# A fused attention and two-MoE kernel: attention's 1206 steps in another written-out order, with some steps on another engine

## The chip, the cores and the metric

The kernel runs on one NeuronCore of a Trainium2 chip, as one program in one launch. The core has five engines that run side by side, each working through its own queue of instructions in order: TensorE (PE in the profile; PEld is its weight load), VectorE (DVE), ScalarE (ACT), GpSimd (POOL) and SyncE (SP, which here only starts transfers). An engine goes on when the semaphores that its next instruction waits for have been raised by the others. The metric is the device time of one execution in microseconds (us); lower is better.

## What is computed

```
scores = q @ k.T / sqrt(D), causal mask       # B=4, H=8, S=576, D=64, all fp32
local  = softmax(scores) @ v
q_p    = phi(q)                               # elu(q) + 1
mem    = (q_p @ M_prev) / (q_p . z_prev + 1e-6)
a      = g * mem + (1 - g) * local            # g = sigmoid(beta) of each head
x = a as [2304 tokens, 512]
x = leaky_relu(x @ w_in) @ w_out              # 512 -> 2048 -> 512, slope 0.01
x = (x @ w_a * (x @ w_b)) @ w_out2            # 512 -> 1536 -> 512
```

## The kernel before

The two MoE layers do every fp32 product as three products of split operands: a high part and a low part of each side, and high x high + high x low + low x high are summed (`three`, lines 286 to 288). They run over groups of 256 hidden columns and over the tokens in two parts (1024 and 1280), and what stands in them is not touched by the change. The change lies in `attention`, which runs first.

**Attention.** It works on 16 pairs of heads, called w = 0 to 15; two pairs in a row (w even and odd) share the work called phi. For each pair:

- `scores` (L578) multiplies q and k of two heads at once. D is 64, so each head takes half of TensorE's rows: the array stands in a mode of 64 rows. Blocks of 128 queries have 128, 256, 384 or 512 keys. `scores_tail` (L606) does the last 64 queries of two pairs in a mode of 64 x 64.
- `least` (L586, L616) on VectorE adds the mask and takes the row minimum of the negated scores out of PSUM; `exp_of` (L532) on ScalarE makes the exponentials and their sum; `recip` (L543, L547) on VectorE inverts the sums; `norm` (L559), on VectorE or GpSimd, multiplies the probabilities by them and by 1 - g.
- `probs_T` (L637) transposes the probabilities on TensorE with the full array, 128 x 128 at a time, and ScalarE or VectorE copies the result out of PSUM (L336, L338) into the tiles `early`, `late` and `tail`.
- `phi` (L452 to L492) makes q_p and its normalisation for two pairs: a minimum (L452), an exponential (L455), `high` (L458), a product with z (`times`, L463 and L468), its sum (`total`, L473), a reciprocal (L487) and a scaling (L343). `phi_T` (L509) transposes it.
- `pv_memory` (L688) and `pv_local` (L716) sum the memory and the local part in the same PSUM banks; the 28 matmuls of `pv_local` stand in a mode of 64 columns, for two heads side by side. `store` copies the result into `xf`; `halves_of` splits it into the high and low parts `xh` for the first token part.
- Beside these stand the first two weight tiles (`Weights.micro`, four half tiles of nine steps each) and the first four accumulations of the MoE layer (`first`, four steps of three matmuls for each).

**What sets the order.** Each piece of work is a step given to a `Plan` by `add` or `dma`, with the engines that could do it and a cost for each. The order is not computed: the table `ORDER` names all 1206 steps, each with a letter for its engine (A ScalarE, D VectorE, E TensorE, G GpSimd, S SyncE), and `run` issues them in that order; each engine's queue is the sub-sequence with its letter. What the engines then wait for follows from the tiles that a step reads and writes. The costs (`TURN`, `COLD`, `took`, `timed`) only give each step a planned start, and from the planned starts of TensorE's steps `run` works out one thing: how many matmuls on the mask (`spin`, L310, results never read) it puts into TensorE's gaps ahead of the first `pv_local`. Costs flagged `port` belong to VectorE steps that the planner treats as sharing a memory port with GpSimd.

Of the kernel before, what the change touches and what calls it, by code (L numbers as in the profile page):

```python
# [19 lines left out]
B, H, S, D = 4, 8, 576, 64  # L20
# [10 lines left out]
def chunks(pr):  # L31
# [13 lines left out]
COLD = 1400.0, 7000.0  # L45
# [1158 lines left out]
```

## Time and profile before

| | |
|---|---|
| time of three runs | 1036.42, 1037.19, 1037.19 us, median 1037.19 |
| span of the profiled execution (first to last instruction) | 1034.8 us |
| what the median holds beyond the span | 2.4 us |
| attention, up to the first matmul of the layers' own loop | 0 to 204.4 us |
| the two MoE layers | 204.4 us to the end |
| steps on TensorE, VectorE, ScalarE, GpSimd, SyncE in attention | 264, 396, 355, 142, 49 |

The profiled execution's own time is not listed apart from the three runs; its span is. Sums are made on the span, and the 2.4 us between it and the median are added at the end. Busy time is the time in which an engine has an instruction in hand; ends of matmuls are modelled, so TensorE's busy share also holds short waits between matmuls.

### The profile page before, as it was taken

The numbers are of one execution on the slowest core, as the hardware profiler recorded it, in microseconds if no ns is written. First come the engines' busy times: TensorE is split into PE (matmuls) and PEld (weight loads), VectorE is DVE, ScalarE is ACT, GpSimd is POOL, SyncE is SP. The second block draws the span as 40 slices with busy tenths as digits, with TensorE's granted clock in tenths as the row PEclk, the third lists the DMA queues.
The fourth block names the chain that finished last, engine by engine and source line by source line (L and its number), as shares of the span: only waits on it lengthen the run. The fifth ranks groups of instructions, "written<-read, shape, count | busy, mean of one in ns | idle before, by whom it ended". The sixth has DMA issues, their size and how long they took to land.

```text
span 1034.8 us, 14335 instructions
## 1 busy us (share of the span) xinstructions
PE 1025.3 (99%) x5420; PEld 826.8 (80%) x5420; DVE 700.4 (68%) x1377; ACT 394.3 (38%) x910; POOL 360.3 (35%) x325
## 2 busy tenths in 40 slices
PE   9999999999999999999999999999999999999998
PEld 4566666788888888888888888888888888888887
DVE  7999998497675758475666683862963955945334
ACT  6899998564323222222323342412122112211111
POOL 4666675135344444342524031420420421411000
PEclk9999999999999999999999999999999999999999
DMA  7334431112111111111101010210210210200022
GB/s 237 117 103 135 145 125 60 57 47 82 41 62 42 61 41 62 41 47 35 62 23 59 1 61 21 82 41 1 82 42 1 82 42 21 82 21 1 1 82 101
DMA packets 19605, 63.31 MB, mean 61 GB/s; under 512 B 2384, under 2 KB 3152, under 8 KB 19536
## 3 DMA queue, kind: packets, MB, share of 16 engines
q1 hardware_dynamic: 19392, 62.40, 17.6%
q8 instruction: 42, 0.69, 0.3%
q14 instruction: 27, 0.22, 0.1%
q10 hardware_dynamic: 144, 0.00, 0.0%
HBM read 57.68 MB, written 4.72 MB: 60 GB/s over the span
## 4 chain that ended last, share of the span: by engine, by line
PE 92%; DVE 6%; ACT 1%; DMA 0%; POOL 0%; issue 0%; ACTq 0%; DVEq 0%; POOLq 0%
PE b L286 27%; PE b L288 27%; PE b L287 27%; PE b L716 3%; PE b L637 3%; PE b L578 2%; DVE p L586 2%; ACT p L532 1%; PE b L688 1%; PE b L509 1%; DVE phi L458 1%; DVE qraw L463 0%; DVE nr L473 0%; PE b L606 0%; DVE pt L616 0%; DMA raw<-in_kqT 0%
## 5 line engine op out<-in xcount | busy, mean ns | idle before, releaser
L286 PE MATMUL b<-xh,w 128*128 128x512 f32 (+1 forms) x800 | 295.4, 369 | 0.0
L287 PE MATMUL b<-xh,w 128*128 128x512 f32 (+1 forms) x800 | 294.6, 368 | 0.0
L288 PE MATMUL b<-xh,w 128*128 128x512 f32 (+1 forms) x800 | 294.4, 368 | 0.0
L225 POOL TENSOR_TENSOR wa<-wa,w 128x512 f32<-128x512 f32 x64 | 108.7, 1698 | 497.6 <-DVE wh L219 399.8
L288 PEld LDWEIGHTS b<-xh,w 128*128 128x128 f32 x800 | 150.8, 188 | 25.3
L286 PEld LDWEIGHTS b<-xh,w 128*128 128x128 f32 x800 | 150.9, 189 | 24.9
L287 PEld LDWEIGHTS b<-xh,w 128*128 128x128 f32 x800 | 150.9, 189 | 24.9
L214 ACT CAST w<-wa 128x512 fp32r<-128x512 f32 x68 | 42.2, 620 | 224.2 <-DVE wa L206 220.0
L1061 DVE TENSOR_TENSOR gf<-b,gf 128x512 f32<-128x512 f32 (+1 forms) x60 | 38.1, 636 | 125.6 <-PE b L288 125.6
L964 DVE TENSOR_TENSOR hl<-gf,hl 128x512 fp32r<-128x512 f32 (+1 forms) x66 | 51.3, 778 | 76.0 <-ACT hl L963 75.6
L1027 DVE TENSOR_TENSOR xf<-b,xf 128x512 f32<-128x512 f32 (+1 forms) x140 | 87.1, 634 | 19.3 <-PE b L288 17.2
L228 POOL TENSOR_TENSOR w<-wa,wr 128x512 fp32r<-128x512 f32 x66 | 92.1, 1396 | 7.0 <-DVE wa L225 1.4
L963 ACT CAST hl<-gf 128x512 fp32r<-128x512 f32 (+1 forms) x91 | 52.5, 577 | 91.0 <-DVE gf L1061 89.5
L1004 ACT ACTIVATE gf<-b 128x512 f32<-128x512 f32 (+1 forms) x76 | 42.0, 553 | 108.5 <-PE b L288 107.0
L286 PE MATMUL b<-hl,w 128*128 128x512 f32 (+1 forms) x220 | 81.1, 368 | 0.0
L287 PE MATMUL b<-hl,w 128*128 128x512 f32 (+1 forms) x220 | 81.0, 368 | 0.0
L288 PE MATMUL b<-hl,w 128*128 128x512 f32 (+1 forms) x220 | 80.9, 368 | 0.0
L559 POOL TENSOR_SCALAR p<-p,stat,keep 128x384 f32<-128x384 f32 (+3 forms) x92 | 61.2, 678 | 47.6 <-DVE stat L547 22.7
L1059 ACT COPY gf<-b 128x512 f32<-128x512 f32 (+1 forms) x60 | 32.5, 542 | 115.7 <-PE b L288 114.9
L532 ACT ACTIVATE p<-p,stat 128x384 f32<-128x384 f32 (+3 forms) x128 | 71.4, 563 | 7.0 <-DVE stat L586 6.8
L1084 DVE TENSOR_TENSOR xf<-b,xf 128x512 f32<-128x512 f32 (+1 forms) x91 | 60.8, 680 | 18.7 <-PE b L288 18.3
L199 DVE TENSOR_SCALAR wh<-wraw 128x512 uint32<-128x512 uint32 x68 | 63.4, 933 | 0.0
(119 smaller groups left out, 1760.7 us busy)
## 6 DMA issues: line engine op xcount, KB each, us to landing
wraw<-in_w_in SPq DMA_DIRECT2D x16, 512.0 KB, 3.4
wraw<-in_w_out SPq DMA_DIRECT2D x16, 512.0 KB, 3.3
qraw<-in_qn SPq DMA_DIRECT2D x8, 768.0 KB, 6.2
wraw<-in_w_a SPq DMA_DIRECT2D x12, 512.0 KB, 3.4
wraw<-in_w_b SPq DMA_DIRECT2D x12, 512.0 KB, 3.3
wraw<-in_w_o SPq DMA_DIRECT2D x12, 512.0 KB, 3.4
vs<-in_vn SPq DMA_DIRECT2D x16, 320.0 KB, 2.9
raw<-in_kqT SPq DMA_DIRECT2D x16, 288.0 KB, 4.4
```

What stands on the lines that cost most here:

```text
L199: nc.vector.tensor_scalar(u("h"), self.raw[i][:, :, 1], 0x7FFFFFFF, None, ALU.bitwise_and)
L225: (nc.gpsimd if eng == "POOL" else nc.vector).tensor_tensor(t["a"], t["a"], f32(half(0)), ALU.subtract)
L228: (nc.gpsimd if eng == "POOL" else nc.vector).tensor_tensor(half(1), t["a"], t["r"], ALU.add)
L286: nc.tensor.matmul(outp, l_hi, r_hi, start=start, stop=False)
L287: nc.tensor.matmul(outp, l_hi, r_lo, start=False, stop=False)
L288: nc.tensor.matmul(outp, l_lo, r_hi, start=False, stop=stop)
L532: nc.scalar.activation(t, t, AF.Exp, bias=s[:, 0, col : col + 1], scale=-1.0, accum_out=s[:, 1, col : col + 1])
L559: ENG[eng].tensor_scalar(live[p], live[p], stats[w % 3][:, 3, col : col + 1], k, ALU.mult, ALU.mult)
L963: after(1, lambda: nc.scalar.copy(t[:, 0, c], gf))
L964: after(1 if eng is nc.vector else 2, lambda: eng.tensor_tensor(t[:, 1, c], gf, f32(t)[:, 0, c], ALU.subtract))
L1027: nc.vector.tensor_tensor(y[pr][:, dm, c], op[:, 0:n], y[pr][:, dm, c], ALU.add)
L1084: nc.vector.tensor_tensor(y[:, i, c], op, y[:, i, c], ALU.add)
```

## The change

The table `ORDER` is replaced as a whole: the same 1206 steps, in another order, and 158 of them on another engine. The counts go from before to after: VectorE 396 to 411, ScalarE 355 to 315, GpSimd 142 to 167, TensorE 264 and SyncE 49 as before. Of the 144 `norm` steps GpSimd has 111 in place of 101; of `times` 12 of 16 in place of 6, of `low` 6 in place of 2, of `scale` 10 in place of 8. Of the 128 copies of transposed probabilities VectorE has 40 in place of 11, and of the 32 of `phi_T` 10 in place of none. The planner's costs change too; as the order is written out, they act only through the number of mask matmuls, which goes from 30 to 20. The same transfers are issued, in another order on SyncE.

```diff
-COLD = 1400.0, 7000.0
+COLD = 1500.0, 7000.0
+READY = {"ACT": 3700.0, "DVE": 600.0, "PE": 1500.0, "POOL": 3600.0, "SP": 720.0}
 ...
 ORDER = (
-    'S0 A2 D3 S1 D6 S7 G4 D5 S8 S11 S71 E27 S9 S10 D34 S113 D30 A35 E36 D28 A31 D32 A29 E41 D37 D39 A38 D42 A33 '
 ...
+    'S0 S1 S7 S8 S10 A2 S9 S11 S113 S71 D3 G6 G4 E27 D34 A35 D32 E36 D30 A33 D28 A31 D53 D39 A29 D37 D54 A40 E41 '
 ...
         def dma(self, fn, size, r=(), w=(), at=0.0, count=1, behind=()):
-            self.add(fn, {"SP": 630.0 * count if count > 1 else 475.0}, r, w, at, size, behind, count)
+            self.add(fn, {"SP": 550.0 * count if count > 1 else 475.0}, r, w, at, size, behind, count)
 ...
             if self.locks(i, e):
-                self.shared = end
+                self.shared = end - (200.0 if e == "POOL" else 150.0)
 ...
-            free = dict.fromkeys(("ACT", "DVE", "PE", "POOL", "SP"), 600.0)
+            free = dict(READY)
 ...
-                free[e] = done[i] = start[i] + cost[e]
+                free[e] = done[i] = start[i] + cost[e] * (2 if e == "PE" and start[i] < COLD[1] else 1)
 ...
-                    wire = max(wire, start[i] + cost[e] / count + 650.0) + size / (220.0 if count == 1 else 150.0)
-                    done[i] = wire + 900.0
+                    wire = max(wire, start[i] + cost[e] / count + 650.0) + size / 330.0
+                    done[i] = wire + 1000.0
 ...
-                    busy = t + self.steps[i][1]["PE"]
+                    busy = t + self.steps[i][1]["PE"] * (2 if t < COLD[1] else 1)
```

Left out of this cut: in `load_first` the factor 4 in the planned sizes of the first two transfers becomes 9.

**TensorE, behind the second `pv_local`.** These are the rows from the last transposes of the pair w = 1 (`pt`, `phi`) over the scores of w = 3 (L578, two heads in two banks) to the first transposes of w = 2. Before:

```order
L637 MATMUL b_646<-ident,pt_491 128x128 x4
L509 MATMUL b_655<-ident,phi_329 128x128 x4
L578 MATMUL b_663<-raw_93 128x256
L578 MATMUL b_664<-raw_93 128x256
L509 MATMUL b_673<-ident,phi_329 128x128
L578 MATMUL b_678<-raw_93 128x512
L578 MATMUL b_679<-raw_93 128x512
L637 MATMUL b_691<-ident,p_590 128x128
```

After:

```order
L637 MATMUL b_620<-ident,pt_457 128x128 x4
L509 MATMUL b_636<-ident,phi_326 128x128 x4
L578 MATMUL b_648<-raw_93 128x256
L578 MATMUL b_649<-raw_93 128x256
L578 MATMUL b_654<-raw_93 128x512
L578 MATMUL b_655<-raw_93 128x512
L509 MATMUL b_665<-ident,phi_326 128x128
L637 MATMUL b_668<-ident,p_523 128x128
```

The single transpose L509 has moved behind the second score step, so the array changes its mode twice here and not four times. Over the whole of attention the changes go from 117 to 94; up to the second `pv_local` there are 22 in both orders.

**VectorE, around the first `phi`.** These are the rows from the score minima of w = 1 to the second sum of the first phi (`nr` is the normalisation, `qraw` the loaded q with z). Before:

```order
L458 SCALAR_TENSOR_TENSOR phi_249<-qraw_96,phi_249 128x512
L463 TENSOR_TENSOR qraw_96<-phi_249,qraw_96 128x512
L452 TENSOR_SCALAR phi_249<-qraw_96 128x640
L586 ISA p_293,stat_99<-b_233,mask 128x128
L586 ISA stat_99 128x1
L586 ISA p_296,stat_99<-b_244,mask 128x256
L586 ISA stat_99 128x1
L473 TENSOR_REDUCE nr_306<-qraw_96 128x8
L458 SCALAR_TENSOR_TENSOR phi_249<-qraw_96,phi_249 128x640
L463 TENSOR_TENSOR qraw_96<-phi_249,qraw_96 128x512
L468 TENSOR_TENSOR qraw_96<-phi_249,qraw_96 128x128
L473 TENSOR_REDUCE nr_306<-qraw_96 128x10
```

After:

```order
L458 SCALAR_TENSOR_TENSOR phi_209<-qraw_96,phi_209 128x640
L586 ISA p_299,stat_99<-b_261,mask 128x256
L586 ISA stat_99 128x1
L473 TENSOR_REDUCE nr_301<-qraw_96 128x8
L586 ISA p_307,stat_99<-b_287,mask 128x512
L586 ISA stat_99 128x1
L338 COPY late_103<-b_303 128x2x128
L473 TENSOR_REDUCE nr_301<-qraw_96 128x10
L487 RECIPROCAL nr_301<-nr_301 128x18
```

The products L463 and L468 have gone to GpSimd, and a copy out of PSUM (L338) has come from ScalarE.

**VectorE, the end of attention.** These are its last rows before the layers' own loop (L957 is the first of that loop): the last weight half tile (`wh`, `wa`, `wr`, `w`) and the low parts of the first hidden values (`hl`). Before:

```order
L206 SCALAR_TENSOR_TENSOR wa<-wraw,wa 128x512
L343 TENSOR_TENSOR hl_2509<-gf_2497,hl_2509 128x512
L219 TENSOR_SCALAR wh<-wa 128x512
L222 SCALAR_TENSOR_TENSOR wr<-wraw,wh 128x512
L225 TENSOR_TENSOR wa<-wa,w 128x512
L228 TENSOR_TENSOR w<-wa,wr 128x512
L343 TENSOR_TENSOR hl_2509<-gf_2540,hl_2509 128x512
L338 COPY tail_108<-b_2562 64x128
L338 CAST hl_2574<-gf_2566 128x512
L343 TENSOR_TENSOR hl_2574<-gf_2566,hl_2574 128x512
L343 TENSOR_TENSOR hl_2574<-gf_2598,hl_2574 128x512
L957 TENSOR_TENSOR xh<-xf,xh 128x512 x2
```

After:

```order
L206 SCALAR_TENSOR_TENSOR wa<-wraw,wa 128x512
L216 CAST w<-wa 128x512
L219 TENSOR_SCALAR wh<-wa 128x512
L225 TENSOR_TENSOR wa<-wa,w 128x512
L222 SCALAR_TENSOR_TENSOR wr<-wraw,wh 128x512
L343 TENSOR_TENSOR hl_2600<-gf_2580,hl_2600 128x512
L343 TENSOR_TENSOR hl_2600<-gf_2598,hl_2600 128x512
L343 TENSOR_TENSOR hl_2503<-gf_2469,hl_2503 128x512
L228 TENSOR_TENSOR w<-wa,wr 128x512
L957 TENSOR_TENSOR xh<-xf,xh 128x512 x2
```

The sum L228 that finishes the second weight tile, which the loop's first matmuls read, has moved from ahead of three of the four `hl` steps to the very end.

## Rows read from the trace of the kernel before

**Rows 1.** The page: span; in 40 slices TensorE's granted clock, and GB/s.

```profile
span 1034.8 us, 14335 instructions
...
PEclk9999999999999999999999999999999999999999
...
GB/s 237 117 103 135 145 125 60 57 47 82 41 62 42 61 41 62 41 47 35 62 23 59 1 61 21 82 41 1 82 42 1 82 42 21 82 21 1 1 82 101
```

**Rows 2.** Busy time by stretch: from:to, length, then each engine's busy us.

```profile
35.00:60.00 25.00, 24.43 (x188) 16.09 (x184) 24.32 (x81) 22.39 (x67) 16.30 (x21) 1.00 0.37 117
60.00:204.40 144.40, 142.85 (x1082) 96.36 (x1081) 125.36 (x397) 124.19 (x364) 83.97 (x105) 1.00 0.32 105
204.40:1032.00 827.60, 827.14 (x3968) 697.94 (x3966) 523.41 (x805) 223.35 (x407) 245.20 (x166) 1.00 0.13 46
```

**Rows 3.** The chain of waits: start us, us, what stood in it.

```profile
32.03 1.44 DVE pt L559
...
168.17 2.85 PE b L716 x28
...
204.42 0.43 PE b L286
```

**Rows 4.** TensorE in order of time, 20 to 66 us: start us, us, instruction.

```profile
22.93 0.87 PE L716 MATMUL b<-early,vs 128*64 128x256 f32 x8
...
40.66 1.04 PE L637 MATMUL b<-ident,p 128*128 128x128 f32 x8
41.63 1.56 PE L578 MATMUL b<-raw 64*128 64x256 f32 x8
...
45.10 0.87 PE L716 MATMUL b<-early,vs 128*64 128x256 f32 x8
...
63.77 1.04 PE L637 MATMUL b<-ident,p 128*128 128x128 f32 x8
64.64 0.70 PE L688 MATMUL b<-phiT,mz 128*128 128x320 f32 x2
```

**Rows 5.** VectorE's groups, 0 to 204.4 us: xcount | busy us, mean ns | idle before.

```profile
L559 DVE TENSOR_SCALAR p<-p,stat,keep 128x512 f32<-128x512 f32 (+1 forms) x36 | 20.8, 588 | 0.5
...
L473 DVE TENSOR_REDUCE nr<-qraw 128x8 f32<-128x512 f32 (+1 forms) x16 | 11.9, 746 | 0.1
...
L463 DVE TENSOR_TENSOR qraw<-phi,qraw 128x512 f32<-128x512 f32 x10 | 8.2, 816 | 0.3
...
L452 DVE TENSOR_SCALAR phi<-qraw 128x640 f32<-128x640 f32 (+1 forms) x14 | 7.8, 554 | 0.5 <-PE b L509 0.5
...
L559 DVE TENSOR_SCALAR pt<-pt,stat,keept 128x576 f32<-128x576 f32 x7 | 6.3, 905 | 0.0
...
L338 DVE COPY late<-b 128x512 f32<-128x512 f32 (+1 forms) x6 | 3.5, 590 | 0.0
...
L468 DVE TENSOR_TENSOR qraw<-phi,qraw 128x128 f32<-128x128 f32 x7 | 2.0, 282 | 0.0
```

**Rows 6.** Two engines at 32 us, and one line's durations (ns min/median/max).

```profile
31.71 1.44 POOL L463 TENSOR_TENSOR qraw<-phi,qraw 128x512 f32<-128x512 f32 x1 [2.39 <-DVE stat L547]
...
31.95 1.52 DVE L559 TENSOR_SCALAR pt<-pt,stat,keept 128x576 f32<-128x576 f32 x1
...
L559 DVE TENSOR_SCALAR pt<-pt,stat,keept x7: 569/583/1657, 31.9 to 158.2; 128x576 f32<-128x576 f32 x7
```

**Rows 7.** VectorE's last row that the thirteenth `pv_local` needs, in order of time.

```profile
164.54 0.08 DVE L586 DVE_READ_ACCUMULATOR2_ANT stat<- 128x1 f32 x1
```

**Rows 8.** VectorE near the end of attention: the row that finishes the second weight tile.

```profile
195.21 0.69 DVE L228 TENSOR_TENSOR w<-wa,wr 128x512 fp32r<-128x512 f32 x1
```

**Rows 9.** Who waited for whom, 0 to 204.4 us: total us, times, longest.

```profile
PEld b L637 <- POOL p L559: 2.5, 4, 0.8
```

**Rows 10.** The first and a later group of mask matmuls, in order of time.

```profile
1.55 2.74 PE L310 MATMUL b<-mask 128*128 128x512 bf16 x6 [1.55 <-POOL mask L294]
...
9.47 2.33 PE L310 MATMUL b<-mask 128*128 128x512 bf16 x10
```

More of the change, by code (lines that the diff above doesn't have):

```diff
@@ L413, in load_first @@
             rest = lambda _: nc.sync.dma_start(raws[0][:, :, c:S], kqT[0][:, :, c:S])
-            dma(lambda _: nc.sync.dma_start(raws[0][:, :, 0:c], kqT[0][:, :, 0:c]), P * 2 * c * 4, w=["raw0.0"], at=-160)
-            dma(rest, P * 2 * (S - c) * 4, w=["raw0.1"], at=-159)
+            dma(lambda _: nc.sync.dma_start(raws[0][:, :, 0:c], kqT[0][:, :, 0:c]), P * 2 * c * 9, w=["raw0.0"], at=-160)
+            dma(rest, P * 2 * (S - c) * 9, w=["raw0.1"], at=-159)
         def load_quad(u):
```

113 rows, old and new, of the table ORDER are left out of this document.

## The prediction

> **What bounds the kernel now.** I read the stretches first. From 204.4 us on, TensorE is busy 827.14 of 827.60 us [rows 2], and no instruction of that part changes: it counts only by the time at which it can begin. Of attention, the stretch from 60 to 204.4 us has TensorE busy 142.85 of 144.40 us, the stretch from 35 to 60 us 24.43 of 25. These shares hide short waits, since ends of matmuls are modelled, so I then read the chain of waits: up to about 60 us VectorE stands in it (a norm at 32.03, as an example), behind that nearly only TensorE, up to the first matmul of the loop at 204.42 [rows 3]. So there are two regimes. At the start VectorE sets the pace and TensorE fills its gaps with mask matmuls or waits. From about the second or third `pv_local` TensorE sets it, with VectorE close behind: it is busy 24.32 of 25 us in the earlier stretch [rows 2].
>
> As a clock for both orders I use the 16 `pv_local` steps, one for each pair of heads. The first begins at 22.93, the second at 45.10 [rows 4], the thirteenth at 168.17 [rows 3]. For each I follow the dependencies back through the order and count which steps of every engine must be done before it.
>
> **The array modes, -2.3 us.** Eight transposes followed by L688, which keeps the mode, take 64.64 - 63.77 = 0.87 us from start to start; eight followed by scores, which change it, take 41.63 - 40.66 = 0.97 [rows 4]. So a change costs 0.10 us. For the change back no pair of rows stands so clean; I take the same. There are 23 fewer, and all 23 lie behind the second `pv_local`, where TensorE is the bound: 23 x 0.10 = 2.3 us. The bounds are 0 (if each falls where TensorE would have waited anyway) and 2.3; I take 2.3, since the stretch has 1.55 us of open idle time in all [rows 2].
>
> **The start, -4.0 us.** VectorE has 84 steps ahead of the second `pv_local` before and 77 after. Sixteen leave this list: two small copies of the gates, which VectorE did while the first scores were still to come and which cost nothing here, and fourteen others: three norms of `p` (3 x 0.588), two of `pt` (2 x 0.905), three `times` (3 x 0.816, and 2 x 0.282 for the narrow second part of two), two sums (2 x 0.746), one `low` (0.554), one `scale` (0.816, as the product, which it resembles), one copy (0.590) and a reciprocal of 18 columns that I leave out. That is 10.0 us by the groups' means [rows 5]. Nine come in: four norms (2.35), one `times` (0.816) and four copies out of PSUM, three of them narrower than the row's, at most 4 x 0.590 = 2.36. That is 5.5 us, so the list is 4.5 us shorter, and the second `pv_local` could begin at 40.6 in place of 45.10.
>
> Three other engines must allow this. TensorE has 18.0 us of work from the start of the first `pv_local` to the start of the second in either order, counted step by step with durations such as these [rows 4], where it took 22.2; and the first can come some 1.5 us earlier, since VectorE has three steps fewer ahead of it (38 to 35, at 0.6 to 0.8 each some 2 us, of which I keep 1.5). So TensorE allows 22.93 - 1.5 + 18.0 = 39.4: not the limit. ScalarE has 60 steps and then 57: not the limit. GpSimd has 24 and then 31, among them the `times` that VectorE's sums wait for; some of its longer steps will end late in the chain. I keep 4.0 of the 4.5. The bounds are 5.7 (TensorE alone) and 1.5 (only the first `pv_local` comes earlier).
>
> The transfers on SyncE stand in another order too: the first four are the same, the load for w = 2 goes behind two small ones. I cost this at nothing, because w = 2 is first used behind the scores and transposes of w = 0 and 1, near 20 us. If that cover were gone, the price would be the time of those two loads: 0.58 MB at the first slice's 237 GB/s [rows 1], 2.4 us.
>
> **VectorE in the later stretch, +1.2 us.** If the start gives 4.0 us and, of the mode changes, those up to the thirteenth `pv_local` (105 before, 86 after) give 1.9, TensorE wants that step 5.9 us earlier. VectorE's last step for it ended at 164.62 [rows 7], 3.5 us ahead of 168.17. Its list up to there goes from 341 to 347 steps and stays about as long: out go net 12 norms, 6 `times`, 4 `low` and 2 `scale`, 7.1 + 6.6 + 2.2 + 1.6 = 17.5 us by the means [rows 5]; in come net 29 copies and 2 low parts, at most 29 x 0.590 + 2 x 0.816 = 18.7. So by these means VectorE gives 3.5 us and not 5.9: 2.4 missing. Against that stands what its long means are made of. A norm of `pt` takes 0.569 us at best and 1.657 at worst, and the one at 31.95 lasted 1.52 us, up to just behind the end of GpSimd's product (31.71 + 1.44) [rows 6]: the two engines hold each other up when both work from SBUF. The copies that come in read PSUM and their mean, 0.590 for a width of mostly 512, leaves no room for such waits. With fewer exposed steps on VectorE (the planner's `port` steps go from 124 to 101) and more on GpSimd (142 to 167), the product of the two counts is 0.96 of what it was, so I expect no more of these waits in all, but they no longer fall on VectorE alone. I take half of the 2.4, +1.2; the bounds are 0 and +4 (VectorE meets GpSimd at every norm).
>
> **The end of attention, +0.5 us.** What is late next is the last weight tile. Its final sum L228 ended at 195.21 + 0.69 = 195.9 [rows 8], 8.5 us ahead of the loop's first matmul at 204.42. Now it is VectorE's last step. Behind the fifteenth `pv_local`, whose tile the weights overwrite, VectorE has 16 steps, at 0.43 to 0.69 each some 9.5 us, and TensorE has 10.0 us up to the loop and 0.7 more up to the first matmul that reads that sum. GpSimd works on the same values meanwhile. Bounds 0 and 1.5; I take 0.5.
>
> **Mask matmuls, 0.** Ten fewer, all ahead of the first `pv_local`, in gaps. They read nothing that others wait for.
>
> **The sum.** -2.3 - 4.0 + 1.2 + 0.5 = -4.6 us. The span 1034.8 [rows 1] becomes 1030.2; with the 2.4 us to the median of the runs, 1032.6 us.
>
> **A rule against it.** GpSimd's product takes 1.44 us where VectorE's mean is 0.816 [rows 5, 6]. The Trainium skill, GPSIMD Engine Reference, section Engine selection, says that elementwise work with two inputs belongs on VectorE, GpSimd being about twice as slow; this trace agrees at 1.8 times. By the rule alone the six products moved would cost 6 x 0.6 = 3.7 us and the sum would be -0.9, which holds only if GpSimd is in the chain; its share of busy time from 60 to 204.4 us is 83.97 of 144.40 us [rows 2]. It gives the first rival below its chance.
>
> **The rivals.**
> *GpSimd comes late (12%).* It has 25 steps more, long ones between the norms, and the transposes of a pair wait for the last norm. Before, weight loads waited for its norms 4 times, 0.63 us each [rows 9]. If each of the 14 pairs behind the second `pv_local` waits once for so long, 8.8 us come back: +4.2, 1041.4 us. It decides from 0.33 us a pair, and the kernel is slower by more than 0.2% from 0.48. Against it: GpSimd idles 60 of the 144.4 us.
> *VectorE keeps up and the start is TensorE's (14%).* -5.7 - 2.3 = -8.0: 1029.2 us.
> *The start gains only at the first `pv_local` (13%).* The chain then runs over GpSimd's `times` and `scale` to VectorE's sums: -1.5 - 2.3 + 1.2 + 0.5 = -2.1, 1035.1 us.
> *VectorE is the bound to the end (4%).* +4 in place of +1.2: -1.8, 1035.4 us.
> *The clock falls at the start (2%).* The granted clock reads full, 2.4 GHz, in all 40 slices [rows 1]; yet the first six mask matmuls took 0.46 us each and ten at 9.47 us 0.23 [rows 10]. If 20 in place of 30 left TensorE at the slow pace up to the first `pv_local`, some 7 us of its work between 13 us and the first `pv_local` (my count, by the same durations) would double, less 2.3 us of mask matmuls: at most +4.7, which eats the gain: 1037.3. The Trainium skill, TensorE: Matmul & The Clock Gate, Part 1, says that the slow clock is the default and that activity lifts it, so fewer mask matmuls speak against the change; no run here shows it yet.
>
> **How the numbers follow.** The forecast as summed has 55%, with a range of its own from 1030 to 1035. A measurement of this kernel can tell about 0.2%, 2.1 us, from no change, so faster means below 1035.1, slower above 1039.3. The forecast and the second rival lie below, the third and fourth on the edge, the clock between, and of the first rival about three quarters above: faster 76%, same 14%, slower 10%. For 8 in 10 the range reaches from the second rival to what lies beyond the third: 1029 to 1037.
>
> **What would show it.** The second `pv_local` begins near 41 us, VectorE's idle time up to there stays small, and behind it TensorE has 72 changes of mode in place of 95. The thirteenth begins near 163.5. The loop's first matmul stands near 199.8, with VectorE's L228 ending within 1 us of it. I am wrong if waits for GpSimd's norms show ahead of the transposes in most pairs, if the second `pv_local` stays behind 43 us, or if TensorE waits several us for L228.

## The result and the profile after

The changed kernel takes 1027.12 us in the median (four runs, 1026.95 to 1027.51), the kernel before 1036.81 on the same occasions: ratio 0.9911, 95% interval 0.9897 to 0.9925. It is faster, as forecast, but by 9.7 us in place of 4.6, and it falls below the range. The profiled execution of after spans 1025.1 us against 1034.8, so the two traces differ by the whole 9.7 us and can be taken apart.

The stretches of after come first, cut as in [rows 2]: from:to, length, busy us of PE, PEld, DVE, ACT and POOL, granted clock, DMA share, GB/s.

```profile
35.00:60.00 25.00, 25.00 (x197) 16.79 (x196) 23.58 (x87) 22.99 (x72) 19.20 (x25) 1.00 0.34 97
60.00:194.40 134.40, 133.09 (x1033) 91.74 (x1033) 122.71 (x389) 105.30 (x310) 95.76 (x119) 1.00 0.35 109
194.40:1022.30 827.90, 827.51 (x3974) 698.15 (x3970) 523.80 (x807) 223.42 (x407) 245.37 (x166) 1.00 0.14 46
```

The last stretch is as long as before (827.9 against 827.6) and as full. All of the gain lies ahead of it. TensorE is still the busiest engine of the middle stretch, which is 10 us shorter; ScalarE has lost work there (124.19 in [rows 2], now 105.30) and GpSimd has gained some (83.97, now 95.76).

The chain of waits of after, beside [rows 3], comes to TensorE at 24.27 us, where it stood on VectorE up to about 60 before, and is mostly there from then on. The rows are start us, us, what stood in it.

```profile
23.65 0.57 DVE phi L343
...
24.27 0.66 PE b L509 x4
...
74.04 3.25 POOL p L559 x5
```

It leaves TensorE in four places: for ScalarE at 30.0, for VectorE and then GpSimd from 69.5 to 77.3, and for VectorE from 109.4 to 114.4 and from 157.6 to 163.6. Behind the second `pv_local` that is 17 us in all. In before it was 42 of the 159 us there: 30.1 on VectorE (from 84.9 to 101.2, for one), 9.0 on ScalarE and 2.8 on GpSimd. So "nearly only TensorE" in the prediction was too much, although TensorE's open idle time there is only 1.6 us before and 1.3 after.

Four rows of TensorE's order of time in after answer to [rows 4] and to the thirteenth `pv_local` and the first matmul of the loop in [rows 3].

```profile
19.50 0.87 PE L716 MATMUL b<-early,vs 128*64 128x256 f32 x8
...
39.11 0.87 PE L716 MATMUL b<-early,vs 128*64 128x256 f32 x8
...
158.29 0.87 PE L716 MATMUL b<-early,vs 128*64 128x256 f32 x8
...
194.50 0.28 PE L716 MATMUL b<-tail,vs 128*64 128x64 f32 x4
194.71 0.50 PE L286 MATMUL b<-hl,w 128*128 128x512 f32 x1
```

The first `pv_local` begins 3.4 us earlier (22.93 before), the second 6.0 (45.10), the thirteenth 9.8 and the loop 9.6. For the last two the same list of before has 168.10 and 204.35, 0.07 less than the chain in [rows 3]. So 6.0 us were made ahead of the second `pv_local` and 3.65 behind it. I had 4.0 and 0.6.

**Where the 6.0 us came from.** Here is VectorE's busy time (the third busy column) up to its last step that the second `pv_local` needs, cut at the step that the first one needs: before, and then after.

```profile
3.70:23.15 19.45, 18.83 (x109) 9.88 (x109) 15.51 (x62) 12.71 (x41) 7.39 (x11) 1.00 0.82 262
23.15:43.77 20.62, 18.14 (x131) 11.67 (x128) 20.41 (x69) 17.49 (x53) 11.40 (x17) 1.00 0.34 108
sum 40.07, PE 36.96 PEld 21.55 DVE 35.92 ACT 30.20 POOL 18.79; mean PE 18.48 PEld 10.78 DVE 17.96 ACT 15.10 POOL 9.40
```

```profile
3.60:19.54 15.94, 15.79 (x99) 8.21 (x97) 12.77 (x56) 11.20 (x34) 9.58 (x18) 1.00 0.84 271
19.54:36.94 17.40, 16.64 (x127) 10.56 (x125) 16.29 (x63) 16.98 (x53) 14.44 (x17) 1.00 0.58 172
sum 33.34, PE 32.43 PEld 18.77 DVE 29.06 ACT 28.18 POOL 24.02; mean PE 16.21 PEld 9.38 DVE 14.53 ACT 14.09 POOL 12.01
```

In the second stretch VectorE was busy 20.41 of 20.62 us before: it set the pace there. Its work up to the second `pv_local` fell from 35.9 to 29.1 us, by 6.9, where I had 4.5.

**Where the 3.65 us came from.** A list of TensorE's rows of after shows what the changes of array mode around a group of scores cost. Each of these score groups (x is its number of matmuls, the widths are mixed) is followed at once by work of another mode.

```profile
14.69 0.70 PE L578 MATMUL b<-raw 64*128 64x256 f32 x4
15.32 1.09 PE L637 MATMUL b<-ident,p 128*128 128x128 f32 x8
...
24.85 1.13 PE L578 MATMUL b<-raw 64*128 64x512 f32 x4
25.91 0.88 PE L637 MATMUL b<-ident,p 128*128 128x128 f32 x6
...
53.48 1.57 PE L578 MATMUL b<-raw 64*128 64x256 f32 x12
54.98 0.33 PE L509 MATMUL b<-ident,phi 128*128 128x128 f32 x1
...
56.33 2.00 PE L578 MATMUL b<-raw 64*128 64x384 f32 x12
58.25 1.09 PE L637 MATMUL b<-ident,p 128*128 128x128 f32 x8
```

From start to start the four groups take 0.63, 1.06, 1.50 and 1.92 us: steps of 0.43, so 0.43 of work, then twice, three and four times as much, and 0.20 left over in each. The 0.20 comes once for a group, however long it is, so it belongs to the changes and not to the scores. The starts of the single matmuls put half of it behind the group's first two matmuls (0.31 us, where later ones of the same 256 columns take 0.21) and half at the group's end. The first transpose behind a change takes longer too:

```profile
33.51 0.33 PE L509 MATMUL b<-ident,phi 128*128 128x128 f32 x1
33.67 0.60 PE L637 MATMUL b<-ident,p 128*128 128x128 f32 x4
...
34.54 0.38 PE L637 MATMUL b<-ident,p 128*128 128x128 f32 x2
34.76 0.70 PE L688 MATMUL b<-phiT,mz 128*128 128x320 f32 x2
```

It is 0.16 us from start to start for the one right behind scores, and 0.22 for two behind L688, which keeps the mode, so 0.11 each. With the 0.10 of the way in [rows 4], going to scores and back costs 0.35 us; I had taken 0.10 for each way, 0.20 in all. Between the second `pv_local` and the loop the transitions from scores to full-array work fall from 29 to 17 and those back from 26 to 15. Summed over all kinds, each at what the fastest fifth of its kind in five traces takes beyond the same work without a change, the changes cost 16.0 us before and 11.9 after: 4.1 us less. What TensorE waits beyond that rises from 2.2 to 2.7 us, and the two together are the 3.65. This sum is an estimate; `modes_back` below tests it.

### The profile page after: what moved, and what is told of

It reads as the page before. It is cut to its first block, busy times and chain, and to the rows that moved or that the text cites. A ratio compares the mean times of both kernels' runs of the same rounds, so it can differ in the third digit from the quotient of the medians.

```text
span 1025.1 us, 14301 instructions
## 1 busy us (share of the span) xinstructions
PE 1018.1 (99%) x5410; PEld 824.9 (80%) x5410; DVE 697.3 (68%) x1386; ACT 379.6 (37%) x868; POOL 386.1 (38%) x358
## 4 chain that ended last, share of the span: by engine, by line
PE 95%; DVE 2%; DMA 1%; ACT 0%; POOL 0%; issue 0%; SPq 0%; POOLq 0%; DVEq 0%
PE b L286 27%; PE b L287 27%; PE b L288 27%; PE b L637 4%; PE b L716 4%; PE b L578 3%; PE b L688 1%; PE b L509 1%; DMA qraw<-in_qn 1%; PE b L606 1%; DVE pt L616 0%; DVE p L586 0%; POOL p L559 0%; ACT p L532 0%; DVE qraw L463 0%
## 5 line engine op out<-in xcount | busy, mean ns | idle before, releaser
L225 POOL TENSOR_TENSOR wa<-wa,w 128x512 f32<-128x512 f32 x66 | 111.5, 1689 | 485.8 <-DVE wh L219 402.1
L228 POOL TENSOR_TENSOR w<-wa,wr 128x512 fp32r<-128x512 f32 x66 | 91.6, 1387 | 5.0
L1084 DVE TENSOR_TENSOR xf<-b,xf 128x512 f32<-128x512 f32 (+1 forms) x91 | 60.7, 680 | 18.7 <-PE b L288 18.3
L532 ACT ACTIVATE p<-p,stat 128x512 f32<-128x512 f32 (+3 forms) x128 | 71.0, 559 | 5.0 <-DVE stat L586 4.7
L559 POOL TENSOR_SCALAR p<-p,stat,keep 128x128 f32<-128x128 f32 (+3 forms) x95 | 61.3, 658 | 17.5 <-DVE stat L547 15.2
```

The source lines that it names most:

```text
L225: (nc.gpsimd if eng == "POOL" else nc.vector).tensor_tensor(t["a"], t["a"], f32(half(0)), ALU.subtract)
L228: (nc.gpsimd if eng == "POOL" else nc.vector).tensor_tensor(half(1), t["a"], t["r"], ALU.add)
L532: nc.scalar.activation(t, t, AF.Exp, bias=s[:, 0, col : col + 1], scale=-1.0, accum_out=s[:, 1, col : col + 1])
L559: ENG[eng].tensor_scalar(live[p], live[p], stats[w % 3][:, 3, col : col + 1], k, ALU.mult, ALU.mult)
L1084: nc.vector.tensor_tensor(y[:, i, c], op, y[:, i, c], ALU.add)
```

## The experiments

Given for each: the median of the runs, the median of before on the same chip, and the ratio with its 95% interval. The intervals are some 1 to 2 us to either side, so the traces carry the finer numbers.

**Two halves.** `start_new` has the new order up to and with the second `pv_local` (step 168), then what remains in the old order. `rest_new` has it the other way round. Each diff is the piece around the seam.

```diff
 D215 E238 D83 G84 D274 A270 A263 E240 E168
-D272 A275 D319 G86 G85 A273 D325 D323 A239 E243 D242 D276 D286
+S213 G111 G112 S289 G85 S358 D272 G86 A273 D239 A275 A216 D276
```

```diff
 S358 D272 A268 E318 D274 G86 A273 D239 E168
-A275 D215 A216 D276 D277 D281 A199 G278 D325 D323 D217
+A199 D215 A275 D319 D325 D323 E243 D242 D276 D286 D277
```

> The new order up to the second pv_local, and behind it all remaining steps in the old order and on the old engines, with 95 mode changes there. If the gain is two separate gains, one made ahead of the second pv_local (6.0 us by the two traces) and one behind it (3.6 us), the first stays and the second goes: about 1030.8 us, the second pv_local near 39.1 us, the loop's first matmul near 198.4. If the old order behind it could not use an earlier start because VectorE is only 3.5 us ahead at the thirteenth pv_local, no more than 3.5 us stay: 1033.3 us or above.

> The old order up to the second pv_local with its 30 mask matmuls, and behind it all remaining steps in the new order and on the new engines, with 72 mode changes there. If the gains are separate, 3.6 us come: about 1033.2 us, the second pv_local near 45.1, the loop's first matmul near 200.8; of the 3.6 us some 2.2 are 23 mode changes of 0.098 and the rest shorter waits of TensorE. If VectorE in the new order only keeps up because it starts 6.8 us earlier, as my term of +1.2 us for VectorE has it, TensorE waits for it behind the second pv_local and less than 1 us comes: 1036 us or more.

Measured: `start_new` 1032.46 against 1036.64, ratio 0.9967 (0.9955 to 0.9980); `rest_new` 1033.05, ratio 0.9969 (0.9957 to 0.9981). Rows of TensorE in order of time, `start_new` first:

```profile
39.16 0.87 PE L716 MATMUL b<-early,vs 128*64 128x256 f32 x8
...
43.86 0.44 PE L509 MATMUL b<-ident,phi 128*128 128x128 f32 x2 [0.62 <-POOL phi L343]
...
46.35 1.13 PE L578 MATMUL b<-raw 64*128 64x512 f32 x4 [1.15 <-DVE stat L586]
...
199.94 0.50 PE L286 MATMUL b<-hl,w 128*128 128x512 f32 x1
```

```profile
44.19 0.87 PE L716 MATMUL b<-early,vs 128*64 128x256 f32 x8
...
199.62 0.50 PE L286 MATMUL b<-hl,w 128*128 128x512 f32 x1
```

The old start itself comes out 0.9 us earlier here than in the trace of before (44.19 against 45.10). The executions differ in TensorE's pace in the first scores; these are the same eight matmuls before and in `rest_new`:

```profile
4.91 1.65 PE L578 MATMUL b<-raw 64*128 64x256 f32 x8 [0.62 <-DMA raw<-in_kqT]
```

```profile
4.87 0.92 PE L578 MATMUL b<-raw 64*128 64x256 f32 x8 [0.57 <-DMA raw<-in_kqT]
```

In after they take 1.24 us. So of the 6.0 us up to the second `pv_local` some 0.9 us can be that pace and not the change; beside the start of `rest_new` the change gives 5.1. In `rest_new` the way from the second `pv_local` to the loop takes 155.4 us, as in after (155.6) and 3.8 less than before (159.25). So the later gain needs no early start of VectorE, and the rival in its expectation falls. In `start_new` that way takes 160.8 us, 1.5 more than before. The rows show why: TensorE waits 0.62 and 1.15 us right behind the seam, where the two orders do not fit; from the third `pv_local` on the old order keeps the earlier start (it is 3.7 us earlier there, 53.21 against 56.91, and the loop 4.4). The two gains are separate; together (4.2 and 3.6 us by the medians) they miss the 9.7 by about the loss at the seam.

**The mode changes put back.** `modes_back` exchanges eleven neighbouring pairs of TensorE's steps behind the second `pv_local`; 116 changes in place of 94. One of the eleven:

```diff
-E327 E245 A246 A244 D287 D283 G285 E332 G282 E247 D330 A170
+E245 A246 A244 D287 D283 G285 G282 E327 D330 E332 A170
```

(the minus line is `modes_back`: there the scores 327 stand ahead of the transposes 245.)

> The new order with eleven neighbouring pairs of TensorE's steps exchanged behind the second pv_local (a score ahead of transposes, or the other way round), each of which puts two changes of array mode back: 116 in place of 94, no step on another engine. If each change costs 0.1 us on the path, 22 x 0.098 = 2.2 us are lost: 1029.3 us. If they fall in time in which TensorE waits anyway, nothing: 1027.1. Above 1030 the exchanges themselves, by half to one us of delay of the exchanged step, cost more than the changes.

Measured: 1031.49 against 1036.64, ratio 0.9952 (0.9940 to 0.9965), 4.4 us above after: twice what I expected of 0.1 a change. In order of time:

```profile
39.33 0.87 PE L716 MATMUL b<-early,vs 128*64 128x256 f32 x8
...
199.19 0.50 PE L286 MATMUL b<-hl,w 128*128 128x512 f32 x1
```

The way to the loop is 159.9 us, 4.3 more than in after and as long as before (159.25), with every step on after's engine. By the same sum as above the changes cost 15.8 us in place of 11.9, which is 3.85 of the 4.3; the other 0.4 is what TensorE waits beyond that. So 22 changes cost 0.18 each. The Trainium skill, TensorEngine Tiling (Array Packing), section Tiling Modes, says that a change of mode drains the engine, and gives no price; the trace agrees, with 0.35 us for the way to scores and back.

**The engines of the start put back.** `engines_start` gives all 22 steps that changed engine up to the second `pv_local` their old engine; `products_start` only the three `times`, `scale` and `low` (and one `times` the other way); `norms_start` only the nine norms. The mask matmuls are held at after's 20 in all three by a table in place of the planner's count.

```diff
 # engines_start, the first of 22
-... D3 G6 ... G56 G5 ... E114 D65 D51 A88 ... E93 G15 D115
+... D3 D6 ... G56 D5 ... E114 G65 D51 D88 ... E93 D15 D115
 # products_start, all
-G15 G20 G26 G77 G80 D75
+D15 D20 D26 D77 D80 G75
 # norms_start, all
-G137 G142 G145 G209 G212 D65 D138 D139 D207
+D137 D142 D145 D209 D212 G65 G138 G139 G207
```

> The new order with its 20 mask matmuls, but up to the second pv_local each step on the engine of the old order: 22 steps change engine, among them norms, three times, a scale and a low back to VectorE, four copies back to ScalarE. If VectorE's shorter list is what makes the second pv_local earlier (its busy time up to there fell from 36.0 to 29.1 us), it comes back to 42 us or later and the time to 1030 or more. If the start's gain is the ten mask matmuls and the order alone, the second pv_local stays within 1 us of 39.1 and the time at 1027 to 1028.

> The new order with its 20 mask matmuls; of the 22 engine moves up to the second pv_local only those of the wide products are undone: three times, a scale and a low back to VectorE, one times back to GpSimd. By the two traces these six steps are 3.6 us of VectorE's time on the way out (2.48 + 0.73 + 0.39) and 0.63 on the way in, so if VectorE's list sets the start, some 3 us come back: second pv_local near 42, 1030 us. If the norms' waits at the shared port were the cause, less than 1 us comes back: 1028.

> The new order with its 20 mask matmuls; of the 22 engine moves up to the second pv_local only those of the nine norms are undone: five back to VectorE, four back to GpSimd. By the two traces the five were 3.90 us of VectorE's time and the four are 1.76, so if VectorE's list sets the start, 2.1 us come back: second pv_local near 41.2, 1029.2 us. If what counted was taking the products off VectorE, less than 1 us: 1028.

Measured: `engines_start` 1032.69 against 1036.81, ratio 0.9962 (0.9949 to 0.9975); `products_start` 1033.32 against 1036.77, 0.9968 (0.9958 to 0.9977); `norms_start` 1029.96, 0.9940 (0.9927 to 0.9952). For each, in the order `engines_start`, `products_start`, `norms_start`: the row of the second `pv_local`, and the busy time over the two stretches up to VectorE's last step for it (DVE is the third engine).

```profile
44.13 0.87 PE L716 MATMUL b<-early,vs 128*64 128x256 f32 x8
```

```profile
sum 38.97, PE 34.89 PEld 19.66 DVE 34.37 ACT 30.17 POOL 17.05; mean PE 17.45 PEld 9.83 DVE 17.18 ACT 15.09 POOL 8.53
```

```profile
43.60 0.87 PE L716 MATMUL b<-early,vs 128*64 128x256 f32 x8
```

```profile
sum 37.86, PE 34.34 PEld 19.67 DVE 32.83 ACT 28.32 POOL 18.19; mean PE 17.17 PEld 9.84 DVE 16.41 ACT 14.16 POOL 9.10
```

```profile
40.87 0.87 PE L716 MATMUL b<-early,vs 128*64 128x256 f32 x8
```

```profile
sum 35.67, PE 33.44 PEld 19.13 DVE 30.71 ACT 28.99 POOL 24.49; mean PE 16.72 PEld 9.56 DVE 15.35 ACT 14.50 POOL 12.24
```

VectorE's work up to there grows by 5.3, 3.8 and 1.7 us against after's 29.06, and the second `pv_local` comes 5.0, 4.5 and 1.8 us later. The step follows VectorE's list, almost one for one, whichever steps fill it. So the moved engines carry 5.0 of the 6.0 us, the wide products more of it than the norms. `engines_start` has the new order on the old engines, and its 44.13 stands beside the 44.19 of the old order in `rest_new`: the order by itself shows no gain here, and the remaining 1.0 is about the 0.9 by which the old start differs between two executions.

**The engines behind it put back.** `engines_rest` does the same for the 136 steps behind the second `pv_local` that changed engine, with after's order and 20 mask matmuls. A few of them:

```diff
-... A239 E243 D242 ... D224 G353 G347 ... E401 D253 A252 D354
+... D239 E243 A242 ... D224 D353 G347 ... E401 A253 A252 D354
```

> The new order, but behind the second pv_local each step on the engine of the old order: 136 steps change engine (copies back to ScalarE, norms and products back and forth), and TensorE's order with its 72 mode changes stays. If the 3.6 us gained there are the mode changes (11 round trips of 0.30 us by the rows, 3.4 us), at most 1 us is lost: 1028 us. If TensorE follows only because VectorE and ScalarE were given other work, the 3.6 us are lost and more, since the order was not made for these engines: 1031 us or above.

Measured: 1052.07 against 1036.77, ratio 1.0158 (1.0139 to 1.0177): 25 us lost, more than either theory had. The new order behind the second `pv_local` is only good with its engines. That does not make the engines the source of the 3.65 us: `modes_back` keeps the engines and loses all of it. What the run shows is that an order and its engines come as one, so that this experiment could not separate them. Part of the 25 us is a lower clock (last section). Two waits stand out; total us, times, longest, 39 to 194 us:

```profile
POOL p L559 <- DVE stat L547: 26.3, 6, 11.3
...
PEld b L637 <- ACT late L336: 8.7, 14, 2.0
```

In after the first is 11.5 us and the second 2.2 us. So the copies out of PSUM that went back to ScalarE come late for the next weight loads.

**The mask matmuls.** `numbers_old` is the new order with the old planner numbers, which put 37 mask matmuls in place of 20. The three others set the number by a table, step: count.

```diff
 # after_m9
-for _ in range(int((t - busy) / (430.0 if t < COLD[1] else 220.0))):
+for _ in range({27: 7, 36: 2}.get(i, 0)):
 # after_m0
+for _ in range({}.get(i, 0)):
 # before_m17
-for _ in range(int((t - busy) / (430.0 if t < COLD[1] else 220.0))):
+for _ in range({27: 6, 36: 1, 46: 10}.get(i, 0)):
```

> The new order with the old planner numbers, which only set how many mask matmuls stand ahead of the first pv_local: 37 in place of 20. My prediction costs them at nothing: 1027.1 us, within 1 us. If mask matmuls fill time that real work wants, 17 x 0.23 = 3.9 us are lost at most: 1031. If more of them lift the granted clock earlier, the first pv_local comes ahead of 19.5 us and the time falls below 1026.

> The old order and engines, with the first 17 of its 30 mask matmuls; the 13 that stand between the transposes and scores from 12.87 us on are left out. If mask matmuls stand on TensorE's path (17 more of them in the new order brought the first pv_local 3.7 us later), the first pv_local comes 13 x 0.22 = 2.9 us earlier, near 20.0, and the time falls by as much, to 1033.9 us. If VectorE's list is what the second pv_local waits for in the old order, the first comes earlier but the second stays near 45.1: 1036.5 us. My prediction's cost of nothing has both where they were.

> The new order with 9 mask matmuls, those ahead of the first two waves of scores; the 11 behind 8.5 us are left out. On the path they are worth at most 11 x 0.23 = 2.5 us: 1024.6 us. If the transposes behind them wait for VectorE and ScalarE anyway, nothing: 1027.1. If they hold the granted clock up, slower than 1027.5.

> The new order with no mask matmul at all. If they only fill, it gives what after_m9 gives, 1024.6 to 1027.1 us. If they lift the granted clock, the first waves of scores and the first transposes (10.3 us of TensorE's work up to the first pv_local by the new order's rows) run at the slow level and take up to twice as long: the first pv_local some 5 us later, 1030 us or above.

Measured: `numbers_old` 1032.12 against 1036.64, ratio 0.9958 (0.9946 to 0.9971); `before_m17` 1036.72 against 1036.81, ratio 1.0000 (0.9991 to 1.0009); `after_m9` 1027.82, ratio 0.9917 (0.9903 to 0.9931); `after_m0` 1028.57, ratio 0.9925 (0.9912 to 0.9938). After `numbers_old` I thought that mask matmuls had been on TensorE's path before, and that ten fewer were the 3.4 us at the first `pv_local`. `before_m17` refutes this: 13 fewer in the old order change nothing, since TensorE then waits for the same inputs. Its first `pv_local` begins at 21.62 and its second at 43.78, beside 22.03 and 44.19 for the whole old start in `rest_new`. A row of TensorE, where mask matmuls stood before:

```profile
15.17 1.10 PE L637 MATMUL b<-ident,p 128*128 128x128 f32 x8 [1.01 <-POOL p L559]
```

In the new order with 37, 16 stand in one piece, and the transposes of `p` come at 15.30 in place of 11.74, the first `pv_local` at 23.22:

```profile
11.84 3.63 PE L310 MATMUL b<-mask 128*128 128x512 bf16 x16
15.30 0.82 PE L637 MATMUL b<-ident,p 128*128 128x128 f32 x6
```

So they cost nothing as long as they fit the wait, and their full time beyond it. With none at all the score groups of the first pairs run slower: the group of 16 narrow scores takes 2.17 us in `after_m0` and 1.20 in after (rows of TensorE, `after_m0` and then after), and the first `pv_local` begins at 20.65 in place of 19.50.

```profile
9.92 2.17 PE L606 MATMUL b<-raw 64*64 64x288 f32 x16
```

```profile
10.16 1.20 PE L606 MATMUL b<-raw 64*64 64x288 f32 x16
```

That is 1.1 us and not the 5 that I feared: transposes run at the fast pace from about 13 us on without any mask matmul. In the times, `after_m0` is 1.4 us above after: the two intervals overlap, but its fastest run (1027.95) is above after's slowest (1027.51).

**A version that should have been better.** `pv_earlier` moves four `pv_local` steps ahead of the two transpose steps in front of them, and leaves out the last two mask matmuls. One of the four:

```diff
-E455 E525 A562 D373 D608 E527 A529 A560
+E525 E527 A562 D373 D608 A529 A560 E455
```

(the minus line is `pv_earlier`: `pv_local` 455 ahead of transposes 525 and 527.)

> The new order with four pv_local steps (the fifth, sixth, seventh and twelfth) placed two to four transposes earlier, right behind scores, which saves one mode change each, and without the last two mask matmuls. By the rows at most 4 x 0.2 + 0.5 = 1.3 us are gained: 1025.8 us. If the copies that these pv_local read come too late for it, TensorE waits at each for up to 2 us: 1029 us or above.

Measured: 1037.53 against 1036.77, ratio 1.0013 (1.0004 to 1.0023): 10 us lost against after. From the seventh to the eighth `pv_local` it takes 13.7 us (10.6 in after) and from the twelfth to the thirteenth 15.8 (10.9). Weight loads wait for ScalarE's copies 4.8 us in all between 45 and 190 us, 2.6 at most, where after has 2.2 and 0.4 at most (these are those of L637; those of L509 wait 3.0 more). Each transpose behind a moved `pv_local` comes 2.9 us later, and so does its copy; that this is the whole cause is only argued. In the later of the two stretches the granted clock falls as well:

```profile
150.00:170.00 20.00, 17.68 (x133) 11.29 (x133) 15.32 (x51) 14.81 (x45) 11.25 (x13) 0.91 0.11 35
```

There eight matmuls of scores take 2.93 us at 159.97, right behind a wait of 2.32 us, where the same eight take 1.56 in after (at 151.23). My forecast looked at what the moved step reads, and not at who waits for the steps it passes. No run here is faster than after.

## Why the prediction was off

| term | predicted, us | measured, us | from |
|---|---|---|---|
| start, up to the second `pv_local` | -4.0 | -6.0 | 45.10 to 39.11 (-5.1 from the 44.19 of `rest_new`) |
| array modes behind it | -2.3 | -4.1 | sums over the changes |
| VectorE in the later stretch | +1.2 | +0.45 | TensorE's other waits there, whoever caused them |
| end of attention | +0.5 | 0 | loop follows `pv_local` at once |
| sum | -4.6 | -9.65 (spans: -9.7) | 204.35 to 194.71 |

**The two regimes** were read rightly in the main: VectorE to the second `pv_local`, TensorE behind it, though with VectorE in the chain more often than "nearly only TensorE" allows. Both halves of the gain are where the prediction put them.

**The start** was the right mechanism with a wrong size, and this is the first step that failed: "the list is 4.5 us shorter". Step by step in the two traces, what left VectorE's list took some 10 us with the gates' copies (I had 10.0 without them), what came in some 3.9 (I had 5.5), and the steps that stayed took up to 0.8 less. The incoming side was priced by groups' means [rows 5], with which I had the right to say "at most" and not more: the four copies took 0.14 to 0.60 us in place of 0.590 each, the four norms 0.40 to 0.50 in place of 0.588. The two copies of the gates, which I costed at nothing, were some 0.75 of work in the full list. I then cut 4.5 to 4.0 for GpSimd, which was not late, and bounded the gain by 5.7 with TensorE alone. That bound fell too: it stood on a first `pv_local` 1.5 us earlier, and it came 3.4 earlier, since VectorE's work up to that step fell by 2.7 us and since the first scores of before ran slowly (22.03 in `rest_new`).

**The array modes** are the second step that failed: "So a change costs 0.10 us. For the change back no pair of rows stands so clean; I take the same." The change back by itself is about 0.10. What the 0.20 for both ways left out is what the work behind each change pays: 0.10 behind the first two scores of a group and 0.05 at the first transpose behind it. It did stand in the trace of before, in score groups of several lengths (26.13 to 26.77, and 28.03 to 29.09 for twice the work: 0.64 and 1.06 us).

**VectorE in the later stretch** failed as arithmetic. I compared TensorE's wish of 5.9 us, which held the start's 4.0, with a slack of 3.5 and a whole list that "stays about as long", so the start's shortening was lost between two sentences. That list was priced by the same means, 18.7 us in and 17.5 out; in the traces it goes from 35.9 + 113.6 to 29.1 + 113.6 us, 6.9 shorter. The later part, in the trace: busy time of VectorE between its last steps for the second and the thirteenth `pv_local`, before and after.

```profile
43.77:164.62 120.85, 119.27 (x930) 78.09 (x928) 113.59 (x376) 111.66 (x338) 81.31 (x101) 1.00 0.39 126
```

```profile
36.94:157.65 120.71, 120.06 (x965) 80.61 (x961) 113.58 (x388) 105.85 (x318) 92.52 (x121) 1.00 0.41 126
```

113.59 and 113.58 us: behind the start the list is as long as it was. It ends 7.0 us earlier (164.62 to 157.65), and the margin to the thirteenth `pv_local` shrinks from 3.5 us [rows 7] to 0.6: 7.0 + 2.8 is the 9.8 by which that step moved. VectorE keeps up, and there is little left of its margin.

**The end**: L228 ends within 1 us of the loop's first matmul, as named, at 194.39 + 0.68 = 195.07, beside 195.9 in [rows 8]:

```profile
194.39 0.68 DVE L228 TENSOR_TENSOR w<-wa,wr 128x512 fp32r<-128x512 f32 x1
```

TensorE does not wait for it: the loop begins 0.21 us behind the start of the last group of `pv_local`, and its second matmul 0.33 later.

**The rivals.** "VectorE keeps up and the start is TensorE's" (14%, 1029.2) came nearest, and was still short by the price of the modes. GpSimd was not late: weight loads wait for its norms 2.3 us in 4 waits behind 39 us, much as before [rows 9], though the chain passes once over five of its norms (at 74.04). Nor did the rule of the Trainium skill, GPSIMD Engine Reference, section Engine selection, decide the sum: that a product is slower on GpSimd holds here too (1.29 us at 50.91, about 0.7 for the one that came to VectorE), and `products_start` shows that taking the products back loses 4.5 us at the second `pv_local`, because the engine that they come back to is the one that sets the pace. **The mask matmuls** at nothing: right for the old order by `before_m17`, and within 1.1 us for the new one, as long as they fit the waits (`numbers_old`). The transfers at nothing: in after VectorE waits 0.58 us for the first load of `qraw`, up to 10.81, so nearly.

## What to carry to other kernels

Price a step that enters or leaves the list of the pacing engine by rows of its own shape, and keep one ledger for that list from the program's start to each milestone; a slack at a late milestone is to be added to what the list has gained before, not compared with it. Price a change of state on both sides, and in the first work behind it, by groups of different length: what is left over when the work is divided out is the change. An order and the engines it was made for are one thing: taking only one of them over can cost more than the change gains.

## What was not expected of the hardware

**Some long waits of TensorE come with a lower clock behind them.** In `engines_rest` the granted clock falls below full, the 2.4 GHz level, behind some of TensorE's long waits, among them one of 2.37 us that ends at 75.84; behind one of 2.73 us that ends at 104.17 it stays full. Stretches of that run:

```profile
70.00:80.00 10.00, 7.63 (x43) 5.49 (x45) 7.00 (x17) 4.87 (x14) 6.05 (x9) 0.83 0.13 39
...
100.00:110.00 10.00, 6.10 (x53) 3.96 (x53) 9.14 (x15) 6.29 (x19) 3.83 (x3) 1.00 0.26 89
```

The clock reads 0.83 as a mean of 10 us, so part of that stretch was granted the lower level, 1.2 GHz, and it is full again in the next. The stretch with the most idle time, from 100 us, reads 1.00: a wait can cost more than itself, but which ones do, no run here was made to show. The mean over the run is 0.995.

**A load that the planner takes as hidden is nearly not.** The 768 KB load of `qraw` that is issued near 50 us lands late by a different amount from run to run. In after GpSimd takes it up 6.3 us behind its issue (49.52 to 55.80), in `after_m9` 7.6 (50.13 to 57.76) and in `products_start` 8.2 (54.03 to 62.27). GpSimd's row in `after_m9`:

```profile
57.76 1.49 POOL L452 TENSOR_SCALAR phi<-qraw 128x512 f32<-128x512 f32 x1 [1.82 <-DMA qraw<-in_qn]
```

And what TensorE's weight load waits for there, between the third and the fourth `pv_local` (total us, times, longest):

```profile
PEld b L637 <- POOL p L559: 1.1, 1, 1.1
```

In after that wait is absent; in `products_start` it is 1.7 us. The same wait is 1.3 us in `norms_start`, 1.0 in `engines_start` and 1.5 in `after_m0`, and these five lose 0.9 to 1.5 us more at the loop than at their second `pv_local`. It is the clearest place where the first rival (GpSimd late) shows. Why the landing differs was not tried.
